# A Fourier-mixing kernel with its start-up rearranged: an early table piece, fewer dummy matmuls, filter loads on GpSimd's queue, and filter halves exchanged by ScalarE

## The chip, the cores and the metric

The kernel runs on one core of a Trainium2 chip. The metric is the device time of one execution in microseconds (us). Before the change it is 2619.39 us, the median of three runs between 2618.38 and 2620.06 us. TensorE is called PE below, VectorE DVE, ScalarE ACT, GpSimd POOL, and SyncE, which only issues transfers here, SP. Each of SP, ACT and POOL has a queue of its own for the transfers that it issues.

## The reference

The input x holds 8 batches of 3008 rows of 256 channels, all in float32. Each channel of a batch is transformed along its rows, multiplied by a complex filter and transformed back; the result then goes through a two-layer network with a hard-swish between the layers.

```python
X = np.fft.rfft(x, axis=1)                   # x: (8, 3008, 256)
Y = X * (filt_r + 1j * filt_i)[None, :, :]   # filters: (1505, 256)
a = np.fft.irfft(Y, n=3008, axis=1).reshape(24064, 256)
h = a @ w_in                                 # (256, 2048)
g = h * np.clip(h + 3.0, 0.0, 6.0) / 6.0
out = g @ w_out                              # (2048, 256)
```

## The kernel before

The transform of length 3008 is split as 47 times 64. It is done with matmuls: a first step over one factor (for batch 0 `a0_unit`), a second step over the other (`b_unit`), the product with the filters (`f_unit` and `y_unit`), and the way back (`bi_unit`, and after it `n_first` or `n_unit`). The network runs in 47 blocks of 512 tokens, and each block in 8 steps over slices of the 2048 inner columns. The work of batches 1 to 7 is fitted into the steps of the blocks by an explicit plan; only batch 0 is transformed by itself ahead of the first block. The order of every instruction on each engine is the order in which the program is written (`manual_schedule`), and each engine carries out its own in that order. What is changed lies in the stretch ahead of the first block, so that stretch is told here in its order.

1. Loads and dummies (lines 967 to 1026). While the first pieces of x are under way, PE runs two dummy matmuls on a tile of zeros (`keep_warm(2)`; each is one 128x512 float32 product, two passes in the trace). x of batch 0 comes in six pieces (`x0_load`), the table of the first transform step in four (`w0_load`); all go on SP's queue but the table's first piece, which goes on ACT's. Into the same row of SP's queue go the raw words of the weights (`load_bits`: the weights come as 64-bit floats and are converted to float32 on the chip) and then the filters (`table_load`, eight transfers each: four for the real and four for the imaginary part), the tables `wf` and `wi` and the identity matrix for transposes. Transfers share eight completion semaphores in rotation, so that a transfer is issued only when the eighth transfer before it has landed.
2. First transform step (lines 1027 to 1033). Eight times `a0_unit(j)`, for j = 0, 4, ... 28: each is 32 matmul passes on PE, whose results ACT and DVE copy out (from j = 24 on, ACT alone). Ahead of every second unit DVE makes the table's odd half from the even one (`w0_odd`, line 402), and that unit's matmuls wait for it. After j = 4, 12 and 20 come two dummy matmuls each. After j = 24 the first slice of weights is converted (`convert`: eight DVE operations, lines 310 to 338).
3. Six rounds, c = 0 to 5 (lines 1045 to 1058). A round has a `b_unit` on PE, two `f_unit`s on DVE (number 2c and 2c+1), the transposes of the next round (`turn(c + 1)`, on PE, copied out by ACT at line 398), and a `bi_unit` on PE for the pair of the round before, copied out by ACT and stored. An `f_unit` is three multiplications of 128x512 or 64x512 elements on DVE: the spectrum by the filter (line 548), and for the crossed products each half of the spectrum by the other half's filter (lines 549 and 550), since the real filter lies in partitions 0 to 63 and the imaginary one in 64 to 127. In the last round each `f_unit` is followed by a `y_unit`, two additions on DVE. The filters of rounds 0 and 1 lie in tiles of their own (`ft`), those of rounds 2 to 5 in pieces of the space that x of batch 0 took: rounds 2 and 3 in that of x's j = 0 to 7, rounds 4 and 5 in that of j = 8 to 15.
4. From the last round to the first block. `direct(10)` and `direct(11)` are 32 matmul passes of 470 or 94 columns each (line 719) on the results of the last two `y_unit`s; `bi_unit`, `n_first` and ACT's copies give the first tokens, and the first block begins (`plain_up`, line 859). Meanwhile DVE and ACT convert more slices of weights (`convert(3)`, `w_abs`), and go on with it through the first block, of which POOL then forms sums of weight blocks (`w_sums`, line 346).

Of the kernel before, what the change touches and what calls it, by code (L numbers as in the profile page):

```python
# [10 lines left out]
FP32 = mybir.dt.float32  # L11
I32 = mybir.dt.int32
AXT = mybir.ActivationFunctionType
ALU = mybir.AluOpType
# [17 lines left out]
P = 128  # L32
D = 256
B = 8
DFF = 2048
HALF = 64
# [6 lines left out]
TC = 4  # L43
NT = KH // TC
TB = 3
FB = 2
# [127 lines left out]
def kernel(  # L174
# [9 lines left out]
    nc = tc.nc  # L184
# [6 lines left out]
    wf_d = nc.inline_tensor(wf_np, name="wf_t").ap()  # L191
# [9 lines left out]
    def pool(name, bufs, **kw):  # L201
        return ctx.enter_context(tc.tile_pool(name=name, bufs=bufs, **kw))
# [12 lines left out]
    op = pool("op", 2)  # L215
    psF = pool("psF", 2, space=PSUM)
    psU = pool("psU", 1, space=PSUM)
# [3 lines left out]
    wf = const.tile([P, 4, 64], FP32, name="wf")  # L221
# [9 lines left out]
    ft = [ft_all[:, ts(i, TC), :] for i in range(FB)]  # L231
# [8 lines left out]
    st = {}  # L240

    def raw(src, row, ap):
        return bass.AP(tensor=src.tensor, offset=src.offset + row * D, ap=ap)


    def table_load(b, c):
        n = TC if b or c < FB else 2 * TC
        if n == TC:
            t = ft[(b * NT + c) % FB]
            st["ft", b, c] = t  # L250
        else:
            t = x0_at(2 * TC * D * (c // 2 - 1), 2 * TC * D).rearrange("p (k d) -> p k d", k=n)
            for i in range(2):
                st["ft", b, c + i] = t[:, ts(i, TC), :]
        for src, p0 in ((filt_r, 0), (filt_i, HALF)):
            for r in range(2):
                o = p0 + 32 * r
                nc.sync.dma_start(t[o:o + 32:2, :, :].rearrange("p k d -> p (k d)"),
                                  raw(src, c * TC + NA * r, [[2 * NA * D, 16], [1, n * D]]))
                nc.sync.dma_start(t[o + 1:o + 32:2, :, :],  # L260
                                  raw(src, NA * (2 - r) - c * TC, [[2 * NA * D, 16], [-D, n], [1, D]]))

    NCONV = 16

# [16 lines left out]
    def w_before(i):  # L281
        same = [j for j in range(i) if W_AT[j] == W_AT[i]]
        return same[-2] if len(same) > 1 else -1
# [13 lines left out]
    def w_abs(i):  # L297
        words = st["bits", i].rearrange("p (n two) -> p n two", two=2)
        st["high", i] = sp.tile([P, 512], FP32, name="s1")
        nc.scalar.activation(out=st["high", i], in_=words[:, :, 1].bitcast(FP32), func=AXT.Abs)  # L300
        nc.scalar.activation(out=words[:, :, 0].bitcast(FP32), in_=words[:, :, 0].bitcast(mybir.dt.uint32), func=AXT.Copy, scale=2.0 ** -32)
# [75 lines left out]
    def x0_at(o, n):  # L377
        return w_all.rearrange("p a b c m -> p (a b c m)")[:, ds(NP * 14 * P - HC * D + o, n)]
# [5 lines left out]
    def w0_load(j, n, q):  # L384
        o = 1 + j * ATOM if j else 0
        q.dma_start(w0[X0:XR, o:1 + (j + n) * ATOM], w0_d[X0:XR, o:1 + (j + n) * ATOM])

    def x0_load(j, n):
        nc.sync.dma_start(x0[X0:XR, j:j + n, :].rearrange("p j d -> p (j d)"), raw(x[0], j, [[HC * D, XR - X0], [1, n * D]]))

    def zt(dh):
        return (xn.rearrange("p a c n -> p (a c n)"), xs.rearrange("p i j d -> p (i j d)"))[dh]

    def copy(dve, to, ps):
        if dve:
            nc.vector.tensor_copy(out=to, in_=ps)
        else:
            nc.scalar.activation(out=to, in_=ps, func=AXT.Copy)

    def w0_odd(j, n):  # L400
        e = w0[0:XR, ds(1 + j * ATOM, n * ATOM)]
        nc.vector.tensor_scalar(out=w0[0:XR, ds(1 + (HC + j) * ATOM, n * ATOM)], in0=e, scalar1=w0[0:XR, 0:1],
                                scalar2=1.0, op0=ALU.mult, op1=ALU.mult)
# [10 lines left out]
    def turn(c):  # L414
        t = t2p.tile([P, TC, D], FP32, name="t2")
        for v in range(2):
            ps = psU.tile([P, 512], FP32, name=("al", "be")[v])
            for s_ in range(2):
                for dh in range(2):
                    z = zt(dh).rearrange("p (s r x) -> p s x r", s=2, x=NU)[:, s_, 2 * c + v, :]  # L420
                    nc.tensor.transpose(ps[:, ds(s_ * D + dh * P, P)], z, st["start"][:, 0:P])
            copy(False, t[:, 2 * v:2 * v + 2, :].rearrange("p k d -> p (k d)"), ps)
        st["t2", 0, c] = t.rearrange("p (v s) d -> p v s d", v=2)


# [113 lines left out]
    def f_unit(b, i):  # L539
        c, r = divmod(2 * i, TC)  # L540
        ps = st.pop(("ps", b, i))
        f = st["ft", b, c][:, r:r + 2, :]

        pool_, n1, n2 = (hp, "h0", "h1") if b == 0 and i & 2 else (sp, "s1", "s2")
        s1, s2 = (pool_.tile([P, 512], FP32, name=n).rearrange("p (u d) -> p u d", u=2) for n in (n1, n2))

        re, im = slice(0, HALF), slice(HALF, P)
        nc.vector.tensor_tensor(out=s1, in0=ps, in1=f, op=ALU.mult)
        nc.vector.tensor_tensor(out=s2[re], in0=ps[re], in1=f[im], op=ALU.mult)
        nc.vector.tensor_tensor(out=s2[im], in0=ps[im], in1=f[re], op=ALU.mult)  # L550
        st["y", b, i] = s1, s2

    def y_unit(b, i):
# [61 lines left out]
    def g_store(b, i):  # L615
        t = st.pop(("t3", b, i))
        for v in range(2):
            nc.gpsimd.dma_start(g_d[b, :, :, ds(2 * (i + v), 2), :].rearrange("c ri u d -> c ri (u d)"),
                                t[ts(v, 64)].rearrange("p ri u d -> p ri (u d)"))
# [4 lines left out]
    for b in range(B):  # L624
# [4 lines left out]
        n = 0  # L629
# [12 lines left out]
    def pair(i):  # L642
        b, js, o, n = chunks[i]
        return b * HC * NA + o, n
# [65 lines left out]
    def direct(i):  # L710
        if "psn" not in st:
            st["psn"] = {(c, dh): (psO.tile([P, 2, 2, P], FP32, name="po%d" % (2 + dh)).rearrange("p a u m -> p (a u m)")
                                   if c else psF.tile([P, 512], FP32, name="psn", tag="f"))
                         for c in range(2) for dh in range(2)}
        for u in range(2):
            k = 2 * i + u - KH + TC
            for (c, dh), ps in st["psn"].items():
                t, n = c * NJ * TOK, (1 if c else NJ) * TOK
                nc.tensor.matmul(ps[:, 0:n], st["y", 0, i][:, u, ts(dh, P)], st["direct"][k][:, ds(t, n)],
                                 start=k == 0, stop=False, skip_group_check=True)  # L720
# [207 lines left out]
    for b in range(B):  # L928
        for n, m, na in (((0, 6, NA), (6, 16, NA), (22, 9, NA)) if b == 0 else ((0, 16, NA), (16, 15, NA)) if b < B - 1
                         else ((0, 16, NA), (16, 10, NA), (26, 1, SPLIT))):  # L930
            o = b * HC * NA + n * NA
# [35 lines left out]
    with tc.manual_schedule():  # L967
# [16 lines left out]
        def load_bits(most):  # L984
            nonlocal loaded
            while loaded < most and w_before(loaded) < done:
                w_load(loaded, nc.sync)
                loaded += 1

        def convert(n):  # L990
            nonlocal done
            for i in range(n):
                w_conv(done)
                w_conv_2(done)
                done += 1
# [13 lines left out]
        ps = psU.tile([P, 512], FP32, name="al")  # L1009

        def keep_warm(n):
            for i in range(n):
                nc.tensor.matmul(ps, zero[:, P:2 * P], zero, start=True, stop=True)

        keep_warm(2)
        for j, n in (0, 4), (4, 4), (8, 8), (16, 8), (24, 4), (28, 4):
            if j % 8 == 0:
                w0_load(j, 8, nc.sync if j else nc.scalar)
            load_bits(j == 28)
            x0_load(j, n)  # L1020
        nc.sync.dma_start(st["start"][:, 0:P], start_d)
        table_load(0, 0)
        nc.sync.dma_start(wf, wf_d)
        nc.sync.dma_start(wi, wi_d)
        table_load(0, 1)
        load_bits(2)
        for j in range(0, HC, 4):
            if j % 8 == 0:
                w0_odd(j, 8)
            a0_unit(j)  # L1030
            if j in (4, 12, 20):
                keep_warm(2)
            convert(j == 24)
        nc.gpsimd.memset(t4, 0.0)
        for c in range(FB, NT, 2):
            table_load(0, c)
# [8 lines left out]
        for c in range(NT):  # L1045
            for i in (2 * c, 2 * c + 1):
                if i % 2 == 0:
                    b_unit(0, i)
                f_unit(0, i)
                if c == NT - 1:  # L1050
                    y_unit(0, i)
            if c + 1 < NT:
                turn(c + 1)
            if c:
                bi_unit(0, 2 * c - 2)
                (g0_first if c == NT - 1 else lambda i: g_store(0, i))(2 * c - 2)
            if c == 4:
                first_load(0, KH - 3 * TC)
        first_load(KH - 3 * TC, KH - TC)
        for i in 1, 2:  # L1060
            w_abs(i)
        direct(NU - 2)
        direct(NU - 1)

# [17 lines left out]
        half = 0  # L1082
# [28 lines left out]
        for i in range(2, len(chunks)):  # L1111
            k = pair(i)[0] // PAIRS
# [70 lines left out]
        for i in range(len(items) + 1):  # L1183
            up = i < len(items)
            k, p = items[min(i, len(items) - 1)]
# [98 lines left out]
```

## Time and profile before

One profiled execution took 2620.5 us, 1.1 us more than the median of the runs; its span is 2618.7 us.

| Engine | busy, us | share of the span |
|---|---|---|
| PE | 2594.3 | 99% |
| DVE | 2054.6 | 78% |
| ACT | 1291.4 | 49% |
| POOL | 485.6 | 19% |

These shares are averages over stages with different limits. The stretch that the change touches is the first 75 us of the span or so; there the table below counts more than the one above. It comes from the view of the profile by stretches.

| Stretch, us | PE busy | DVE busy | ACT busy | granted PE clock |
|---|---|---|---|---|
| 6.70 to 12.20 | 0.00 | 0.01 | 0.00 | 0.79 |
| 35.00 to 43.00 | 7.31 | 7.56 | 3.41 | 1.00 |
| 43.00 to 51.00 | 8.00 | 7.70 | 4.55 | 1.00 |
| 79.00 to 100.00 | 21.00 | 20.03 | 12.42 | 1.00 |

A matmul's busy time in the trace is modelled, so a PE that is busy throughout need not be the limit; whether it is has to be read from the waits and from the order of time. "Idle before, releaser" in a row of the trace names what the engine had waited for.

### The profile page before, as it was taken

The page shows a single profiled execution, that of the slowest core. Times are in us where ns is not written, and L with a number is a line of the kernel's source. Part 1 is how long each engine was busy: PE and PEld are TensorE (multiplying, and loading weights), DVE is VectorE, ACT ScalarE, POOL GpSimd, SP SyncE. Part 2 cuts the span into 40 slices and gives each one's busy share as a digit, 9 for nine tenths or more (in the row PEclk, how much of TensorE's full clock was granted, in tenths as well). Part 3 has the DMA queues.
Part 4 walks back from the last instruction along what each step waited for, and adds up shares of the span by engine and source line. Part 5 has one row for each costly group of instructions (what it writes and reads, how often), then busy time and mean ns, then how long its engine had stood idle before and what let it go on. Part 6 is the DMA issues. An engine that isn't in the chain of part 4 may idle for free.

```text
span 2618.7 us, 87007 instructions
## 1 busy us (share of the span) xinstructions
PE 2594.3 (99%) x37896; PEld 2044.6 (78%) x37896; DVE 2054.6 (78%) x3616; ACT 1291.4 (49%) x2678; POOL 485.6 (19%) x711
## 2 busy tenths in 40 slices
PE   7999999999999999999999999999999999999999
PEld 4477777778877788788877878778787788888887
DVE  6978867888778886888868888788877888766666
ACT  3554455444544455444554544544445454455554
POOL 2161122111121112211122121211112120111110
PEclk9999999999999999999999999999999999999999
DMA  7742243212332123421224113341133321110000
GB/s 210 216 118 68 57 110 109 66 35 70 88 109 70 33 76 82 113 66 33 84 75 122 56 33 86 79 117 54 40 80 88 109 57 48 51 44 20 23 22 26
DMA packets 130419, 199.25 MB, mean 76 GB/s; under 512 B 21698, under 2 KB 97952, under 8 KB 129718
## 3 DMA queue, kind: packets, MB, share of 16 engines
q1 hardware_dynamic: 114925, 149.15, 20.3%
q0 software_dynamic: 14720, 44.16, 6.1%
q8 instruction: 297, 4.87, 0.8%
q14 instruction: 84, 0.69, 0.1%
q10 hardware_dynamic: 393, 0.39, 0.1%
HBM read 121.35 MB, written 83.98 MB: 78 GB/s over the span
## 4 chain that ended last, share of the span: by engine, by line
PE 93%; DVE 3%; POOL 1%; issue 0%; DMA 0%; ACT 0%; SPq 0%; POOLq 0%; DVEq 0%; ACTq 0%
PE po L752 43%; PE al L752 24%; PE be L752 18%; PE psn L692 2%; PE psf L528 1%; PE psf L469 1%; PE psf L587 1%; PE be L587 1%; POOL w_all L346 1%; PE be L469 1%; DVE g L805 1%; DVE y L312 0%; PE psn L752 0%; DVE y L335 0%; DVE w_all L338 0%
## 5 line engine op out<-in xcount | busy, mean ns | idle before, releaser
L752 PEld LDWEIGHTS po<-w_all,g 128*64 128x64 f32 x20808 | 1232.5, 137 | 247.0 <-issue 12.8
L752 PE MATMUL po<-w_all,g 128*64 128x128 f32 (+1 forms) x20808 | 1406.9, 274 | 1.4 <-DVE g L805 0.7
L800 ACT ACTIVATE r<-h,half_c 128x512 f32<-128x512 f32 x736 | 531.0, 722 | 345.1 <-DVE h L781 333.0
L752 PE MATMUL al<-xt,w_all 128*64 128x256 f32 x4416 | 664.1, 379 | 2.4 <-POOL w_all L346 2.3
L805 DVE SCALAR_TENSOR_TENSOR g<-r,h 128x512 f32<-128x512 f32 x736 | 535.6, 729 | 143.6 <-ACT r L800 128.5
L752 PE MATMUL be<-xt,w_all 128*64 128x256 f32 x2944 | 442.6, 379 | 0.0
L781 DVE TENSOR_TENSOR h<-be,s 128x512 f32<-128x512 f32 x368 | 254.0, 690 | 132.3 <-PE be L752 101.9
L747 POOL TENSOR_TENSOR xt<-xn 128x256 f32<-128x256 f32 x184 | 150.5, 837 | 892.5 <-ACT xn L674 892.5
L752 PEld LDWEIGHTS be<-xt,w_all 128*64 128x64 f32 x2944 | 211.2, 137 | 106.5
L752 PEld LDWEIGHTS al<-xt,w_all 128*64 128x64 f32 x4416 | 278.9, 137 | 3.7 <-POOL w_all L346 3.4
L795 ACT ACTIVATE h<-al 128x256 f32<-128x256 f32 x368 | 141.0, 383 | 274.5 <-PE al L752 273.1
L813 DVE TENSOR_TENSOR g<-g 128x512 f32<-128x512 f32 x367 | 261.3, 712 | 12.6
L786 DVE TENSOR_TENSOR h<-al,s 128x256 f32<-128x256 f32 x368 | 156.1, 424 | 137.8 <-PE al L752 132.8
L776 ACT ACTIVATE s<-al 128x256 f32<-128x256 f32 x368 | 141.3, 384 | 207.5 <-PE al L752 207.5
L752 PE MATMUL al<-xn,w_all 128*64 128x256 f32 (+1 forms) x1536 | 240.1, 393 | 1.1 <-DVE g L805 0.7
L752 PE MATMUL be<-xn,w_all 128*64 128x256 f32 (+1 forms) x1536 | 236.4, 388 | 0.0
L767 ACT ACTIVATE s<-be 128x256 f32<-128x256 f32 x368 | 141.1, 383 | 170.2 <-PE be L752 170.2
L812 DVE TENSOR_TENSOR g<-g 128x256 f32<-128x256 f32 x367 | 165.4, 451 | 12.5
L766 ACT ACTIVATE s<-al 128x256 f32<-128x256 f32 x368 | 141.4, 384 | 59.3 <-PE al L752 59.3
L818 DVE TENSOR_TENSOR g<-g 128x256 f32<-128x256 f32 x367 | 162.4, 442 | 2.4
L752 PEld LDWEIGHTS be<-xn,w_all 128*64 128x64 f32 x1536 | 110.3, 137 | 62.3 <-issue 7.1
L494 POOL DMA_DIRECT2D z_tmp<-t x144 | 71.8, 506 | 321.6 <-ACT s L767 296.0
(159 smaller groups left out, 1763.4 us busy)
## 6 DMA issues: line engine op xcount, KB each, us to landing
t<-g_tmp SPq DMA_DIRECT2D x184, 120.0 KB
t<-z_tmp SPq DMA_DIRECT2D x42, 512.0 KB
g_tmp<-t POOLq DMA_DIRECT2D x68, 256.0 KB, 4.3
z_tmp<-t POOLq DMA_DIRECT2D x120, 144.0 KB, 3.3
o_tmp<-o SPq DMA_DIRECT2D x46, 256.0 KB
xs<-in_x_dram SPq DMA_DIRECT2D x60, 192.0 KB
ft<-in_filt_r_dram SPq DMA_DIRECT2D x176, 64.0 KB
ft<-in_filt_i_dram SPq DMA_DIRECT2D x176, 64.0 KB
```

The source lines that it names most:

```text
L747: nc.gpsimd.tensor_tensor(out=o, in0=x0, in1=x1, op=op_)
L752: nc.tensor.matmul(ps[ds(o, STRIP)], w[:, ds(o, STRIP)], x, skip_group_check=True, **kw)
L766: nc.scalar.activation(out=s[:, 0, :], in_=al, func=AXT.Copy)
L767: nc.scalar.activation(out=s5, in_=be[:, 1, :], func=AXT.Copy)
L776: nc.scalar.activation(out=s[:, 1, :], in_=al, func=AXT.Copy)
L781: nc.vector.tensor_tensor(out=st["h"][0].rearrange("p (a n) -> p a n", a=2), in0=be, in1=s, op=ALU.add)
L786: nc.vector.tensor_tensor(out=st["h"][1][:, 256:512], in0=al, in1=s5, op=ALU.add)
L800: nc.scalar.activation(out=r, in_=st["h"][i], func=AXT.Relu, bias=half_c, scale=1.0 / 6.0)
L805: nc.vector.scalar_tensor_tensor(out=st["g", k, p][:, o:o + 2, :].rearrange("p a n -> p (a n)"), in0=st["r", i], scalar=1.0, in1=st["h"][i ...
L812: v.tensor_tensor(out=g[:, G1, :], in0=g[:, G3, :], in1=g[:, G22, :], op=ALU.add)
L813: v.tensor_tensor(out=g[:, G3:G2 + 1:2, :], in0=g[:, G3:G1 + 1, :], in1=g[:, G11:G11 + 1, :].broadcast_to([P, 2, 256]), op=ALU.subtract)
L818: nc.vector.tensor_tensor(out=g[:, G4, :], in0=g[:, G12, :], in1=g[:, G2, :], op=ALU.subtract)
```

## The change

There are six edits.

- The table's first piece goes on SP's queue, ahead of all of x, instead of on ACT's.
- The first raw weights are asked for ahead of x's fifth piece instead of its sixth, and their conversion stands after `a0_unit(20)` instead of after `a0_unit(24)`. `wf` is asked for ahead of the first filters instead of after them.
- The dummy matmuls after j = 4 and 12 are one each instead of two, those after j = 20 are gone, and one stands after j = 24. Two new ones stand ahead of `direct`.
- The imaginary filters of rounds 2 to 5 are loaded through POOL's queue, and the filters of rounds 2 and 3 now take the space of x's j = 16 to 23.
- Of round 0's two copies after the transposes, DVE makes the second.
- For rounds 4 and 5 ACT copies the filters with their halves exchanged into the `ft` tiles that rounds 0 and 1 have left (`swap`, in rounds 2 and 3), and their `f_unit`s then need one multiplication of 128x512 in place of the two of 64x512.

```diff
@@ table_load
-            t = x0_at(2 * TC * D * (c // 2 - 1), 2 * TC * D).rearrange("p (k d) -> p k d", k=n)
+            t = x0_at(2 * TC * D * (3 - c // 2), 2 * TC * D).rearrange("p (k d) -> p k d", k=n)
...
         for src, p0 in ((filt_r, 0), (filt_i, HALF)):
+            q = nc.gpsimd if p0 and n > TC else nc.sync
             for r in range(2):
                 o = p0 + 32 * r
-                nc.sync.dma_start(t[o:o + 32:2, :, :].rearrange("p k d -> p (k d)"),
+                q.dma_start(t[o:o + 32:2, :, :].rearrange("p k d -> p (k d)"),
...
+    def swap(c, half):
+        f, t = st["ft", 0, c], ft[c % FB]
+        st["tf", 0, c] = t
+        for o in half:
+            copy(False, t[ds(HALF - o, HALF), :, :], f[ds(o, HALF), :, :])
@@ turn
-            copy(False, t[:, 2 * v:2 * v + 2, :].rearrange("p k d -> p (k d)"), ps)
+            copy(c == 0 and v == 1, t[:, 2 * v:2 * v + 2, :].rearrange("p k d -> p (k d)"), ps)
@@ f_unit
         nc.vector.tensor_tensor(out=s1, in0=ps, in1=f, op=ALU.mult)
-        nc.vector.tensor_tensor(out=s2[re], in0=ps[re], in1=f[im], op=ALU.mult)
-        nc.vector.tensor_tensor(out=s2[im], in0=ps[im], in1=f[re], op=ALU.mult)
+        if ("tf", b, c) in st:
+            nc.vector.tensor_tensor(out=s2, in0=ps, in1=st["tf", b, c][:, r:r + 2, :], op=ALU.mult)
+        else:
+            nc.vector.tensor_tensor(out=s2[re], in0=ps[re], in1=f[im], op=ALU.mult)
+            nc.vector.tensor_tensor(out=s2[im], in0=ps[im], in1=f[re], op=ALU.mult)
@@ the stretch ahead of the first block
-                w0_load(j, 8, nc.sync if j else nc.scalar)
-            load_bits(j == 28)
+                w0_load(j, 8, nc.sync)
+            load_bits(j == 24)
             x0_load(j, n)
         nc.sync.dma_start(st["start"][:, 0:P], start_d)
+        nc.sync.dma_start(wf, wf_d)
         table_load(0, 0)
-        nc.sync.dma_start(wf, wf_d)
...
             a0_unit(j)
-            if j in (4, 12, 20):
-                keep_warm(2)
-            convert(j == 24)
+            if j in (4, 12, 24):
+                keep_warm(1)
+            convert(j == 20)
...
+            if c in (2, 3):
+                swap(c + 2, (0, HALF))
...
+        ps = psU.tile([P, 512], FP32, name="al")
+        keep_warm(2)
         direct(NU - 2)
         direct(NU - 1)
```

## The prediction

> **What bounds the kernel now.** First the page: its chain of work that ended last is PE for 93%, nearly all in the network. The six edits lie in the first 62 us, so what counts is whether time won there reaches the point from which PE runs without a break. I read the timeline of that stretch, the table by stretches, the waits, and the chain up to 200 us.
>
> ```profile
> PE 93%; DVE 3%; POOL 1%; issue 0%; DMA 0%; ACT 0%; SPq 0%; POOLq 0%; DVEq 0%; ACTq 0%
> ...
> DVE w_all L402 <- DMA w_all<-w_t: 7.7, 1, 7.7
> ...
> 6.70:12.66 5.96, 0.00 (x1) 0.00 (x1) 0.42 (x1) 0.00 (x0) 2.39 (x2) 0.77 1.03 244
> 12.66:17.39 4.73, 4.73 (x65) 4.61 (x65) 0.56 (x1) 0.98 (x2) 0.00 (x0) 0.57 1.03 275
> ```
>
> The first line is the page's chain, the second a wait, the others rows by stretch (PE, weight loads, DVE, ACT, POOL, granted clock, DMA share, GB/s). PE idles 6 us because DVE waits 7.7 us for the table's first piece, and then starts at clock 0.57.
>
> ```profile
> 12.66 4.80 PE L752 MATMUL po<-w_all 112*64 112x96 f32 x64 [5.96 <-DVE w_all L402]
> 17.39 1.98 PE L1013 MATMUL al<-r 128*128 128x512 f32 x4
> 19.30 2.86 PE L752 MATMUL po<-w_all 112*64 112x96 f32 x64
> ...
> 55.90 0.69 DVE L550 TENSOR_TENSOR s<-po,w_all 64x512 f32<-64x512 f32 x1
> 56.63 0.69 DVE L548 TENSOR_TENSOR h<-po,w_all 128x512 f32<-128x512 f32 x1
> 57.35 0.68 DVE L549 TENSOR_TENSOR h<-po,w_all 64x512 f32<-64x512 f32 x1
> 58.05 0.69 DVE L550 TENSOR_TENSOR h<-po,w_all 64x512 f32<-64x512 f32 x1
> 58.77 0.69 DVE L559 TENSOR_TENSOR t<-h 64x512 f32<-64x512 f32 x1
> 59.49 0.69 DVE L560 TENSOR_TENSOR t<-h 64x512 f32<-64x512 f32 x1
> ```
>
> In the timeline, two units of the first step cost 4.80 us cold and 2.86 warm, a warm dummy pair 1.98, and PE has no gap until the transposes at 31.50. The rounds are DVE's: three multiplications at a pitch of 0.715 us, without a gap, six per round (4.29 us; PE needs 4.10).
>
> ```profile
> 57.72:60.28 2.56, 0.00 (x0) 0.03 (x1) 2.45 (x5) 0.60 (x1) 0.00 (x0) 1.00 0.49 130
> 60.28:63.56 3.28, 3.28 (x8) 1.92 (x9) 3.17 (x5) 2.34 (x4) 0.00 (x0) 0.62 0.31 74
> 63.56:66.05 2.49, 2.49 (x9) 1.43 (x9) 2.28 (x5) 0.00 (x0) 0.00 (x0) 0.81 0.88 180
> 66.05:68.08 2.03, 2.03 (x11) 1.21 (x10) 1.96 (x4) 0.00 (x0) 1.13 (x2) 1.00 1.05 378
> ...
> 75.23 0.69 DVE L331 TENSOR_TENSOR y<-g,y 128x512 f32<-128x512 f32 x1 [2.03 <-ACT g L301]
> ...
> 130.67 36.46 POOL L346 TENSOR_TENSOR w_all<-w_all 128x128 f32<-128x128 f32 x64 [16.38 <-DVE w_all L338]
> ```
>
> PE waits 2.56 us for `y_unit(10)`, its clock drops, and the four equal quarters of `direct` take 3.28, 2.49, 2.03 and 2.11 us. At 75.23 DVE waits for ACT, which is behind PE's end of `direct`; from there DVE converts weights almost without a gap to 130.5, POOL's 64 subtractions follow that, and then PE. So a shift of the end of `direct` passes to the end of the kernel.
>
> **The change part by part**, on the profiled execution's 2620.5 us.
>
> *Start of the first step.* The trace's landing events show x's first two pieces at 5.3 and 6.6 us, x's j = 8 to 15 at 11.2, j = 16 to 23 at 14.8, the table's fourth piece at 15.4, the raw weights at 18.6, x's last at 20.1; the table's first piece, 3% of the bytes, came at 12.3. Put first, it lands near 4, and the other pieces move by at most its 0.6 us (148 KB at 244 GB/s). Units 0 and 4 then start when the first dummies end, at 6.7. From there: unit 8 at 11.3 (its x), units 8 and 12 2.86, one dummy 0.95, units 16 and 20 2.86: PE is done at 18.0.
>
> *The moved conversion.* In the changed program's order on DVE its eight operations stand ahead of `w0_odd(24)`, which stood ahead of them before. DVE's copy ends at 18.5; the raw weights, now one piece earlier, land at 17 to 18; the eight operations took 27.72 to 32.11, 4.39 us; `w0_odd` 0.41. So unit 24 starts at 23.3 although its x is there by 19: PE idles 5.3 us, and the nearest rows (idle 5.96, then 0.57) say that it resumes cold. Units 24, dummy, 28 cost 1.43 + 0.95 + 1.43 = 3.8 us warm, 2.40 + 1.84 + 2.40 = 6.6 cold (the cold pair of dummies at 3.02 took 3.68). Before, the clock was back 4 to 5 us after PE resumed, so I take 2.40 + 1.84 + 1.4 = 5.6. The transposes start at 28.9 instead of 31.5: -2.6 us, between -1.6 and -4.4.
>
> *DVE's copy in round 0.* ACT's second copy starts 0.50 after its first and takes 0.60; DVE's of that shape takes 0.69 and can start no earlier: +0.1. DVE is free there.
>
> *The exchanged halves.* Four steps lose a multiplication; three of them lie ahead of `y_unit(10)`: 3 x 0.715 = -2.1 us at `direct`'s start. Step 11 wins a fourth, but its result (63.8 before) is needed only halfway through `direct`. ACT pays four copies of 64x1024: by its rows of 256 columns (0.384) and 512 (0.597) each is 1.02 us. In rounds 2 and 3 they add 2.04 to some 2.3 us of copies, against a round of 4.29. Behind them on ACT stand the transposes' copies, for which `b_unit` waits; these come 0.9 us later than before, but `b_unit` ran 3 us ahead of DVE in rounds 4 and 5. Cost nothing; without that cover up to 2 us.
>
> *Filters on POOL's queue.* Eight issues leave SP (0.64 each, 5.1 us), and what follows there is asked for that much earlier. POOL had nothing between 9.1 and 42.1; by its issue rows of 0.5 to 0.65 us its eight are done within 6 us of unit 20's end, and the nearest landings, 3 to 6 us, put the filters there by 30. `swap` wants them at 43, `f_unit(4)` at 41. Nothing, and at most 1 us either way by contention. `wf` and the raw weights' place in the queue: nothing, wanted 10 us later.
>
> *Dummies.* Those after 4, 12 and 24 are in the sums above; the pair after 20 lay on the path and is in the difference. The two ahead of `direct` start when the last round's `bi_unit` ends, 1.4 us ahead of `y_unit(10)`'s new end, and run 1.9: `direct` starts at most 0.5 later, 0.1 by the timeline. If they keep the clock, `direct` takes four times 2.03 instead of 9.91: -1.8 us (between -1.8 and 0).
>
> The Trainium skill ("TensorE: Matmul & The Clock Gate", section "HAM oscillation — how this bites in real kernels") wants no PE gap of over about 3.4 us. By that the gap of 2.56 us would throttle nothing, the pair would be worth nothing, and the sum would be 1.8 us smaller; the clock of 0.62 behind that gap says otherwise, and I go by it.
>
> *What is late next.* On DVE alone 75.23 could move by 2.5 + 2.9 + 2.03 = 7.4 us, on the way over PE and ACT by 2.6 - 0.1 + 2.1 - 0.1 + 1.8 = 6.3; the smaller holds. Raw weights for the following conversions landed 5 to 10 us before use, and the transfers for `n_first` 4.8 us ahead, of which 2.4 are used up.
>
> Sum: 2620.5 - 6.3 = 2614.2 for such an execution; it stood 1.1 above the median, so 2613.1 for the median.
>
> **Rivals.** *Nothing of the start is left.* PE stays cold to the transposes, or the filters on POOL's queue delay the conversion: the first term shrinks to -1 or less, and the direct pair brings half: -3.5, 2615.9. For it: the 5.3 us hole is the change's own. Against it: eight microseconds of slack on x's last piece before.
>
> *The gain is lost on the way.* From 64 to 72 the DMA engines are 100% busy; if the loads behind `direct` set the pace, only half arrives: -3, 2616.4. Against it: no wait for a load of raw weights shows before 79.
>
> *More at the start.* The clock survives or returns at once: 3.8 instead of 5.6, and the total is -8.1: 2611.3.
>
> *Slower: the clock stays down in the rounds.* With fewer dummies PE comes cold out of the hole and the rounds' gaps keep it so. A round of 4.10 at 4.80/2.86 is 6.9 us, 2.6 over DVE's; five rounds cost 13, against 6.3: +7, 2626. It decides once the share of PE's work in a round (62% between 31.50 and 34.00, with clock 1.00) is too little to lift the clock from cold. Against it: it was lifted at 17 while PE worked without a break, as it does from 23.3.
>
> **How the numbers follow.** Forecast 0.60 (2611.8 to 2614.8 for its own terms), more at the start 0.12, start lost 0.09, lost on the way 0.09, slower 0.10. Likeliest 2613.1. The range runs from 2610.5, below the better start, to 2617, above both lost cases. About 0.2%, 5.2 us, is what a measurement can tell: the limit is 2614.2. Of the forecast about a seventh lies above it, of the lost cases nearly all: faster 0.65, same 0.25, slower 0.10.
>
> **What would show it.** After: the wait for the table's first piece gone and units 0 and 4 at about 6.7; PE idle from 18 to 23 behind `w0_odd`; transposes at about 28.9; two multiplications a step in rounds 4 and 5, four ACT copies of about 1.0 us; `direct` near 8.1 us with clock 1.00; POOL's 64 subtractions at about 124.4 instead of 130.67. I'm wrong if ACT waits for filters in `swap`, if PE's clock is below 1 in the rounds, or if the start of POOL's subtractions moves much less than the end of `direct`.

## The result: 2614.8 us, and the profile after

The changed kernel takes 2614.78 us (median of 20 runs between 2613.59 and 2616.06). The kernel before took 2619.06 on the same chip (20 runs between 2617.88 and 2620.49). The ratio is 0.9983 with a 95% interval from 0.9976 to 0.9990: 4.3 us won, 0.17%. The two profiled executions lie further apart, 2620.5 and 2613.62, which is 6.9 us; what the traces suggest for that difference stands further down. The page's chain of work that ended last, after:

```profile
PE 96%; DMA 2%; DVE 1%; SPq 0%; issue 0%; ACT 0%; POOL 0%; POOLq 0%; DVEq 0%; ACTq 0%
```

DVE's share of the chain fell from 3% to 1%. The table by stretches of the changed kernel has PE, weight loads, DVE, ACT and POOL with their busy time, then the granted clock, the DMA share and GB/s:

```profile
17.64:23.18 5.54, 0.00 (x2) 0.03 (x1) 5.06 (x10) 0.00 (x0) 4.70 (x8) 0.71 1.09 226
23.18:28.89 5.71, 5.71 (x66) 4.38 (x66) 0.00 (x0) 1.47 (x3) 0.00 (x0) 0.68 0.94 185
31.50:53.50 22.00, 21.28 (x176) 9.17 (x176) 20.15 (x30) 14.14 (x23) 4.56 (x8) 1.00 0.86 263
...
55.63:63.80 8.17, 8.17 (x34) 4.81 (x32) 7.65 (x14) 2.38 (x4) 0.00 (x0) 1.00 0.50 131
```

PE idles 5.54 us behind the moved conversion (the hole, in what follows) and comes back at a clock of 0.68 (first two lines). In the rounds the clock is 1.00, and so it is in `direct` (last line), where it had been 0.62 and 0.81 in the first two quarters. The timeline of the same execution:

```profile
6.57 2.86 PE L762 MATMUL po<-w_all 112*64 112x96 f32 x64
...
22.46 0.41 DVE L409 TENSOR_SCALAR w_all<-w_all 112x384 f32<-112x384 f32 x1
23.18 2.83 PE L762 MATMUL po<-w_all 112*64 112x96 f32 x32 [5.54 <-DMA ft<-in_filt_i_dram]
...
43.49 2.13 ACT L405 ACTIVATE ft<-w_all 64x1024 f32<-64x1024 f32 x2
...
53.81 1.98 PE L1023 MATMUL al<-r 128*128 128x512 f32 x4
55.63 1.74 PE L729 MATMUL psn<-w_all,t 128*128 128x470 f32 x4
...
124.08 36.40 POOL L353 TENSOR_TENSOR w_all<-w_all 128x128 f32<-128x128 f32 x64 [16.21 <-DVE w_all L345]
```

Units 0 and 4 run at 6.57 instead of 12.66. Unit 24 (23.18) is cold and takes 2.83 us, because `w0_odd(24)` comes only at 22.46, behind the eight operations of the conversion. The releaser that the line names, a filter transfer, isn't it: unit 24 multiplies what `w0_odd` wrote, and starts 0.3 us behind its end, as it does (0.2 us) in the other kernels with this order. POOL's 64 subtractions start at 124.08 instead of 130.67.

Where the time went in this pair of executions, as shifts of the same landmark: first transpose 31.50 to 28.89 (-2.61); end of `y_unit(10)` 60.18 to 55.02 (-5.16); end of `direct` 70.20 to 63.80 (-6.40); end of POOL's subtractions 167.13 to 160.48 (-6.65); span -6.9. So in this pair what is won ahead of the first block arrives, and nothing in the 2450 us behind it gives any back.

### The profile page after: what moved, and what is told of

Its sections match the earlier page's. It is cut to its first block, busy times and chain, and to the rows that moved or that the text cites. A ratio compares the mean times of both kernels' runs of the same rounds, so it can differ in the third digit from the quotient of the medians.

```text
span 2611.8 us, 87014 instructions
## 1 busy us (share of the span) xinstructions
PE 2590.7 (99%) x37894; PEld 2042.8 (78%) x37894; DVE 2050.0 (78%) x3613; ACT 1294.1 (50%) x2681; POOL 491.1 (19%) x719
## 4 chain that ended last, share of the span: by engine, by line
PE 96%; DMA 2%; DVE 1%; SPq 0%; issue 0%; ACT 0%; POOL 0%; POOLq 0%; DVEq 0%; ACTq 0%
PE po L762 44%; PE al L762 25%; PE be L762 18%; PE psn L702 2%; PE psf L535 1%; PE psf L476 1%; PE psf L597 1%; PE be L597 1%; DMA w_all<-in_x_dram 1%; PE be L476 1%; PE psf L581 0%; DMA out_dram<-o 0%; PE psf L762 0%; PE psf L449 0%; DVE g L815 0%
```

## The experiments

My theory was the prediction's sum: the start, the exchanged halves and the dummies ahead of `direct` bring some 2 us each, and the hole ahead of unit 24 costs some. The rivals were that the halves or the dummies bring nothing by themselves, that the hole costs nothing because the filters are late anyway, and that POOL's queue carries part of the gain. In the table each kernel stands beside the kernel before on the same chip, in runs taken in turn with its own.

| Kernel | median us (runs) | before, same chip | difference | ratio, 95% interval |
|---|---|---|---|---|
| changed kernel | 2614.78 (20) | 2619.06 | -4.3 | 0.9976 to 0.9990 |
| conv24 | 2612.06 (8) | 2619.45 | -7.4 | 0.9962 to 0.9982 |
| hole_warm | 2614.31 (11) | 2619.45 | -5.1 | 0.9971 to 0.9988 |
| no_direct_dummies | 2614.90 (11) | 2619.45 | -4.6 | 0.9972 to 0.9990 |
| table_first | 2616.35 (11) | 2619.45 | -3.1 | 0.9979 to 0.9997 |
| no_swap | 2617.29 (11) | 2619.77 | -2.5 | 0.9980 to 0.9997 |
| no_swap_no_dummies | 2619.06 (11) | 2619.77 | -0.7 | 0.9987 to 1.0004 |
| sp_filters | 2615.65 (11) | 2619.77 | -4.1 | 0.9975 to 0.9993 |
| imag_all_pool | 2615.28 (11) | 2619.77 | -4.5 | 0.9973 to 0.9991 |
| conv24_nod | 2611.75 (7) | 2620.02 | -8.3 | 0.9959 to 0.9981 |
| best2 | 2610.10 (5) | 2620.02 | -9.9 | 0.9951 to 0.9978 |
| best3 | 2608.76 (5) | 2620.30 | -11.5 | 0.9943 to 0.9970 |

The intervals reach 2 to 3 us to either side, so a difference of 1 to 3 us between two of the changed kernels is read from the landmarks in their traces; the medians alone can't settle it. two_halves, with a single run, is not in the table.

Unless it says otherwise an edit is made to the changed kernel.

### conv24: the conversion back behind unit 24

```diff
-            convert(j == 20)
+            convert(j == 24)
```

> The changed kernel, but the first conversion again behind a0_unit(24), so that w0_odd(24) stands ahead of it on DVE. If the moved conversion makes the hole in PE (17.64 to 23.18 us), unit 24 starts when its x has landed, at 19.3 us, unit 28 at about 21, the transposes at about 23 instead of 28.9; f_unit(0) is then held by the first filters, which land at 27.9, and starts at 28 instead of 32.7: about 4.2 us less than the changed kernel, some 2610.5. If it is the late x or the transfers that make the hole, unit 24 stays at 23 and the time at 2614.8.

The hole is gone, and the kernel is about 3 us faster than the changed one by the medians (-7.4 beside -4.3, with intervals that overlap); in its trace POOL's subtractions start 2.4 us earlier (121.70 against 124.08). The timeline shows what came in its place:

```profile
19.54 1.54 PE L762 MATMUL po<-w_all 112*64 112x96 f32 x32 [1.65 <-DMA w_all<-in_x_dram]
...
29.03 0.69 DVE L555 TENSOR_TENSOR s<-po,ft 128x512 f32<-128x512 f32 x1 [2.95 <-DMA ft<-in_filt_r_dram]
...
41.30 2.13 ACT L405 ACTIVATE ft<-w_all 64x1024 f32<-64x1024 f32 x2 [1.92 <-DMA w_all<-in_filt_r_dram]
```

Unit 24 starts at 19.54 as its x lands, warm. The transposes come at 23.53 instead of 28.89, 5.4 us earlier, but `f_unit(0)` starts only 3.7 us earlier: it now waits 2.95 us for filters. `swap` waits 1.92 us for filters too, and from `f_unit(0)` to the end of `y_unit(10)` it takes 23.43 us instead of 22.31. So the hole cost something, less than its length, and less than the 4.2 us expected here.

### table_first: one edit alone, on the kernel before

```diff
-                w0_load(j, 8, nc.sync if j else nc.scalar)
+                w0_load(j, 8, nc.sync)
```

> The kernel before, with only the table's first piece put at the head of SP's queue. Units 0 and 4 start at 6.6 us, the transposes at about 23.6 instead of 31.5; f_unit(4) then waits for the filters of rounds 2 and 3, which landed at 38.4 before: all in all some 5.2 us less than the kernel before, 2613.9. By the forecast's account of the start (2.6 us with the moved conversion) this one edit is worth more than in the changed kernel; if the rival holds that the start's gain is lost on the way, the time stays within 1 us of 2619.1.

This line alone brings 3.1 us by the medians, beside the change's 4.3, where 5.2 had been expected. The pair of traces does show 5.3 at the start of POOL's subtractions (125.35 against 130.67), but this trace is one of the fastest runs of its kernel, and the one before stands above its median. The transposes come at 24.02, 7.5 us earlier than before the change, against 2.6 with all six edits. Part of it is lost again to a wait for filters in the second round, in DVE's timeline:

```profile
38.46 0.69 DVE L548 TENSOR_TENSOR s<-po,w_all 128x512 f32<-128x512 f32 x1 [2.21 <-DMA w_all<-in_filt_r_dram]
```

### hole_warm: five more dummies in the hole

```diff
             a0_unit(j)
+            if j == 20:
+                keep_warm(5)
```

> The changed kernel with five more dummy matmuls after a0_unit(20), some 4.8 us of work in PE's hole. If the slow clock behind the hole is what makes units 24 and 28 and their dummy take 5.7 us, they take 3.8 us with clock 1.00 and everything after comes 1.9 us sooner: 2612.9. If the clock does not matter there (copies or transfers set the pace), nothing changes. If the clock's own phase is what spreads the runs of one kernel by 2.5 us, the spread gets smaller.

Units 24 and 28 run warm: from the start of unit 24 to the transposes it takes 4.00 us, with clock 1.00, instead of 5.71. But unit 24 itself started at 24.16 instead of 23.18 in this execution, so the transposes come at 28.16 instead of 28.89. Beside the kernel before, the median is only 0.8 lower than the changed kernel's, which can't be told from nothing, and the spread is no smaller (2612.55 to 2615.80). In its profile the clock drops at another place, at 145.7 us; the section on the hardware comes back to that.

### no_direct_dummies: the pair ahead of direct taken out

```diff
-        ps = psU.tile([P, 512], FP32, name="al")
-        keep_warm(2)
         direct(NU - 2)
```

> The changed kernel without the two dummy matmuls ahead of direct. By the forecast's term direct takes 9.9 us instead of 8.17 and starts 0.5 us sooner: +1.2 to +1.8 us in a profiled run, 2616.3. If the drop of the clock seen before the change hangs on where the gap falls in the clock's own period, only part of the runs pay: +0.5 us in the median and a wider spread. If the drop was chance, 0.5 us faster.

The median is the same (2614.90 and 2614.78). In the table by stretches, the wait ahead of `direct` and `direct` itself:

```profile
55.30:56.56 1.26, 0.02 (x3) 0.04 (x1) 1.20 (x3) 0.60 (x1) 0.00 (x0) 1.00 1.00 249
56.56:64.80 8.24, 8.24 (x34) 4.88 (x34) 7.78 (x13) 2.39 (x4) 0.00 (x0) 1.00 0.41 107
```

`direct` keeps a clock of 1.00 and takes 8.24 us without any dummy. PE's wait ahead of it is 1.26 us here, and was 2.56 before: the exchanged halves had already shortened it.

### no_swap and no_swap_no_dummies: without the exchanged halves

```diff
-            if c in (2, 3):
-                swap(c + 2, (0, HALF))
```

and, in the second, also the edit of no_direct_dummies. The results are computed in the old way, with three multiplications a step.

> The changed kernel without the exchanged halves: rounds 4 and 5 have three multiplications a step again. If they are worth 0.95 us a step (2.145 against 1.20 us, as the changed kernel's rows stand), the end of y_unit(10) moves by 2.8 us, but direct started 0.6 us after it and now follows at once: 2.3 us slower, 2617.1. If they are worth the forecast's 0.715 a step, 1.6 us slower, 2616.4. The two dummies now fill a gap of 2.6 us; direct takes 8.2 us.

> The changed kernel without the exchanged halves and without the two dummies ahead of direct. If the dummies' gain hangs on the length of the gap, the gap of 2.6 us drops the clock in a part of the executions: in a profile where it does, direct takes 9.9 us instead of 8.2, and the median is 0.5 to 1.5 us above the run without the halves alone, while without the dummies alone it cost nothing (gap 1.3 us). If the forecast's account is right and the dummies as such bring 1.8 us, it is 1.8 us slower than the run without the halves alone.

`y_unit(10)` ends 28.82 us behind the first transpose in no_swap and 26.12 in the changed kernel, 2.7 us or 0.90 a step; the medians give 1.8. Without the halves the wait ahead of `direct` is back, and there the dummies bring 1.8 us by the medians and 1.3 in the two traces. In the timeline of the kernel with neither:

```profile
59.42 2.17 PE L729 MATMUL psn<-w_all,t 128*128 128x470 f32 x4 [2.56 <-issue]
...
62.18 2.75 PE L729 MATMUL psn<-w_all,t 128*128 128x470 f32 x4
...
65.19 1.77 PE L729 MATMUL psn<-w_all,t 128*128 128x470 f32 x4
```

Behind 2.56 us of idle time the groups of 470 columns take 2.17, 2.75 and then 1.77 us, and `direct` 9.91. So each of the two edits alone kept `direct` warm in its trace; the second adds nothing.

### two_halves: what the exchanged halves save

```diff
-            nc.vector.tensor_tensor(out=s2, in0=ps, in1=st["tf", b, c][:, r:r + 2, :], op=ALU.mult)
+            for h_ in re, im:
+                nc.vector.tensor_tensor(out=s2[h_], in0=ps[h_], in1=st["tf", b, c][h_, r:r + 2, :], op=ALU.mult)
```

> The changed kernel, but in rounds 4 and 5 the multiplication of 128x512 by the exchanged filters is split into two of 64x512, each with both operands in the same partitions. If the pitch of 0.72 us came from the crossed partitions of the kernel before, the two go at 0.60 us and y_unit(10) ends 0.6 us per step later than in the changed kernel, near 56.9 for three steps. If it comes from operations that use half the partitions, they go at 0.72 and it ends near 57.9, and with the 58.1 of the kernel without exchanged halves. The view to read is the pitch of the multiplications in rounds 4 and 5.

Its one run took 2618.12 us, and `y_unit(10)` ends at 57.63, near the second of the two values. DVE's timeline:

```profile
50.16 0.69 DVE L555 TENSOR_TENSOR s<-po,w_all 128x512 f32<-128x512 f32 x1
50.77 1.38 DVE L558 TENSOR_TENSOR s<-po,ft 64x512 f32<-64x512 f32 x2
52.18 0.69 DVE L555 TENSOR_TENSOR s<-po,w_all 128x512 f32<-128x512 f32 x1
```

The first half follows the full multiplication after 0.61 us, the second half its predecessor after 0.69, and the next full one after 0.73: 2.02 a step, against 2.14 before and 1.20 with one multiplication. Neither theory is right as I put it: the first half has half the partitions and yet comes after 0.61, and the second has aligned operands and comes after 0.69.

### sp_filters: all filters on SP's queue again

```diff
-            q = nc.gpsimd if p0 and n > TC else nc.sync
+            q = nc.sync
```

> The changed kernel with all filters on SP's queue. The filters of rounds 4 and 5 are asked for up to 41.4 us and land at about 44, and the exchange on ACT, which began at 43.5, waits up to 1 us; b_unit runs 3 us ahead, so the forecast's nothing holds: within 0.5 us of 2614.8. If the cover is too thin: ACT's wait comes through, up to 2 us slower.

4.1 us beside 4.3, and from `f_unit(0)` to the end of `y_unit(10)` 22.32 us beside 22.31: POOL's queue brings nothing that these runs can tell.

### imag_all_pool: all imaginary filters on POOL's queue, on top of conv24_nod

```diff
-            q = nc.gpsimd if p0 and n > TC else nc.sync
+            q = nc.gpsimd if p0 else nc.sync
-            convert(j == 20)
+            convert(j == 24)
-        ps = psU.tile([P, 512], FP32, name="al")
-        keep_warm(2)
```

> The first conversion behind a0_unit(24), no dummies ahead of direct, and all imaginary filters on POOL's queue, those of rounds 0 and 1 too. With the conversion moved alone, f_unit(0) waited 2.95 us and the exchange on ACT 1.92 us for filters. If SP's row of filter issues is what delays them, both waits go or shrink below 1 us and the time falls by 1 to 2 us to about 2610.5; if the bytes as such set the pace (x's last piece comes later instead), it stays at 2612.

It is 3.8 us slower than conv24_nod when each stands beside the kernel before on its own chip. Two things went wrong. POOL's `memset` of a tile, which runs at 7.08 in the changed kernel, now stands behind eight DMA issues, and beside it DVE's `w0_odd(8)` takes 3.58 us instead of 0.41, from the timeline (the three first lines). And the edit also caught the filters of later batches, whose eight issues, 4.1 us, now stand in the middle of POOL's subtractions (the three last):

```profile
10.16 3.58 DVE L409 TENSOR_SCALAR w_all<-w_all 112x384 f32<-112x384 f32 x1
...
11.26 2.25 POOL L1044 MEMSET t<- 128x2560 f32 x1
...
13.95 1.39 PE L762 MATMUL po<-w_all 112*64 112x96 f32 x14 [3.26 <-POOL t L1044]
...
122.25 4.84 POOL L353 TENSOR_TENSOR w_all<-w_all 128x128 f32<-128x128 f32 x9 [16.21 <-DVE w_all L345]
127.04 0.52 POOL L259 DMA_DIRECT2D ft<-in_filt_i_dram  x1
...
131.12 31.78 POOL L353 TENSOR_TENSOR w_all<-w_all 128x128 f32<-128x128 f32 x55
```

The subtractions end at 162.91, 4.5 us later than in conv24 (158.37), although they begin only 0.55 later.

### conv24_nod, best2 and best3: what the experiments point to

conv24_nod joins the edits of conv24 and no_direct_dummies. best2 adds the imaginary filters of rounds 0 and 1 on POOL's queue, for batch 0 alone and behind those of rounds 2 and 3 (one load of four transfers), which wait for unit 20 (`table_load` gets an argument for which of the two filters it loads):

```diff
-            q = nc.gpsimd if p0 and n > TC else nc.sync
+            q = nc.gpsimd if p0 and b == 0 else nc.sync
...
-        table_load(0, 0)
+        table_load(0, 0, (0,))
...
-        table_load(0, 1)
+        table_load(0, 1, (0,))
...
-        for c in range(FB, NT, 2):
-            table_load(0, c)
+        table_load(0, FB)
+        for c in range(FB):
+            table_load(0, c, (1,))
+        table_load(0, FB + 2)
```

best3 issues only the first of these four transfers ahead of those of rounds 0 and 1, and the other three behind them.

> The changed kernel with the conversion of the first weights back behind a0_unit(24) and without the two dummies ahead of direct. If those dummies only delay direct by half a microsecond (direct started 0.62 us behind y_unit(10) with them and 0.10 without), it should come out at 2611.6, 0.5 below the 2612.06 with the dummies. If they do keep the clock up when PE comes without the hole ahead of the rounds, direct takes up to 1.8 us more and the time is about 2613.4. The view to read is the granted clock in direct: 1.00 by the first, below by the second.

> As the run above, and the imaginary filters of rounds 0 and 1 go through GpSimd's queue too, but behind those of rounds 2 and 3, which wait until unit 20 has left its x; so they cannot compete with x's earlier pieces, and the real filters of round 0 have four transfers less ahead of them or between them on SyncE's queue. With the order of the queue as the cause of the 2.95 us wait of f_unit(0), that wait shrinks to 1 us or less and f_unit(0) starts at 27.2 instead of 29.0: 2610.0, 1.6 below the run above. With the bytes as the cause (the 16 queues are busy for 0.86 to 1.09 of that stretch) f_unit(0) stays at 29, and the time at 2611.6, or later where the imaginary filters now come last. The view to read is the first multiplication of f_unit(0) and what it waits for.

> The version at 2610.1 with another order on GpSimd's queue: one transfer of the imaginary filters of round 2 first (it waits for unit 20, and holds the queue until then), then the imaginary filters of rounds 0 and 1, then the rest of round 2. In that version those of round 0 were issued from 20.93 us on, and f_unit(0) started at 27.94 behind a wait of 2.50; here they are issued some 2.5 us earlier. If their place in the queue sets f_unit(0), it starts near 25.8 and the time is about 2608.3 beside 2610.1. If the bytes set it (the queues are busy throughout, and the real filters and the next raw weights come in the same stretch), f_unit(0) stays within 0.5 us of 27.9 and the time at 2610. The view to read is the first multiplication of f_unit(0) and the waits of the six units behind it.

The three medians came within 0.5 us of what was expected: 2611.75, 2610.10 and 2608.76. In conv24_nod `direct` ran with clock 1.00 in 8.24 us. From the first transpose to `f_unit(0)` it is 5.49 us in conv24, 5.04 in best2, which still waits 2.50 us for a transfer, and 3.81 in best3, as in the changed kernel, where PE alone set it (3.81). The start of `f_unit(0)` does not decide between the two accounts by itself: 27.48 is within the 0.5 us of 27.9 that stood for the bytes. The landings do. The last of the four transfers of round 0's imaginary filter lands at 27.57 in best2, and the wait ends with it; in best3 it is issued 0.6 us earlier and lands at 25.17. So its place in the queue was the cause. In best3 that wait is no longer one for a transfer (the first line is best2's, and the raw weights that it names aren't what `f_unit(0)` needs; the others are best3's, DVE and PE):

```profile
27.94 0.69 DVE L555 TENSOR_TENSOR s<-po,ft 128x512 f32<-128x512 f32 x1 [2.50 <-DMA bits<-in_moe_w_out_dram]
```

```profile
27.48 0.69 DVE L557 TENSOR_TENSOR s<-po,ft 128x512 f32<-128x512 f32 x1 [1.27 <-PE po L537]
...
61.11 1.84 PE L764 MATMUL psn<-wai,t 128*64 128x94 f32 x40 [1.17 <-DMA t<-g_tmp]
```

`f_unit(0)` now waits for PE, not at 25.8 as expected but at 27.48, since unit 4 started at 9.04 in this execution and 7.68 in best2's. And there is a new wait: `n_first` waits 1.17 us for the tokens' way through memory, which the prediction had seen 4.8 us ahead; `direct` ends 11.4 us earlier than before by now. best3 is the fastest version measured, 11.5 us under the kernel before and 6 to 7 under the changed one, though its interval and best2's overlap.

## Why the prediction was right, point by point

The likeliest time was 2613.1, the range 2610.5 to 2617.0, and 2614.78 lies inside it. It lies just outside the limit of 0.2% (2614.2): the kernel is faster, since the interval lies wholly below 1, but by less than the bound that "faster", with 0.65, was given for, and inside the one of "same", with 0.25. On the pair of profiled executions the sum, -6.3, stands beside a shift of `direct`'s end of -6.40. That it comes so near is luck in part: two terms were mis-sized, in opposite directions (+0.6 us on the halves, -0.4 on the start of `direct`), and the 1.8 us of the dummies came by another edit.

- **Start, -2.6.** In the pair -2.61, with the hole of 5.54 us (5.3 forecast), the cold unit 24, and the transposes at 28.89 (28.9). The four other kernels that are the same up to there had the transposes at 29.15, 29.31, 30.32 and 30.49 (sp_filters, the same but for the queue of the filters, at 30.48). The median of the first five is 29.31, so about -2.2 is typical, inside the range given; how much the start of the kernel before varies is not known, since it has one trace. The landing times in the prediction stand some 0.25 us late against the timeline (DVE's wait for the table's first piece, put at 12.3, had ended by 12.19), so that unit 8, forecast at 11.3, ran at 10.74; at unit 24 0.1 us of it was left.
- **DVE's copy in round 0, +0.1.** From the transposes to `f_unit(0)` 3.68 before, 3.81 after: +0.13.
- **Halves, 3 x 0.715 = -2.1.** This is the first term that was mis-sized. It measured 2.7 in the traces: a step goes from 2.14 to 1.20 us. What failed is "three multiplications at a pitch of 0.715 us": I took the pitch as a property of each multiplication, and it isn't, as the last section shows. The cover of ACT's copies held; two take 2.13 us, and no `b_unit` came late for them.
- **Filters on POOL's queue: nothing.** sp_filters agrees, within what its runs can tell.
- **Dummies ahead of `direct`, -1.8.** This is the second. `direct` went from 9.91 to 8.17 us as forecast, but the step "If they keep the clock, `direct` takes four times 2.03 instead of 9.91" gave the gain to the wrong edit. I had noted that the halves shorten PE's wait, and not asked what the clock does behind the shorter wait. no_direct_dummies shows that it stays at 1.00, and no_swap_no_dummies that without the halves the dummies would have earned most or all of their 1.8. In the changed kernel they only delay `direct`, which starts 0.62 us behind `y_unit(10)` (0.1 forecast).
- **What is late next.** The shift passed to POOL's subtractions whole (124.08; 124.4 forecast), and no load behind `direct` took it. That such a wait exists a few us further on, best3 shows.
- **From the pair to the median.** The forecast took off 1.1 us, since the profiled execution of before stood so far above its median. The executions differ by 6.9 us and the medians by 4.3: before's profile stands 1.4 above the median of the 20 runs and after's 1.2 below. The likeliest time is 1.7 us too low, most of it for this reason. The last section gives the cause that the traces point to.

Three of the rivals did not come: the clock was 1.00 in the rounds, the shift arrived whole, and the clock did not survive the hole. Of the fourth, "nothing of the start is left", a grain was true: table_first wins 7.5 us at the transposes, and the moved conversion gives back 5 of them. I had costed the hole only against the kernel before, where PE was late anyway, and so didn't see that the edit which makes it is the change's worst; taking it out was worth 2.4 us in the traces and 3 by the medians.

## What to carry to other kernels

Ask of each protective edit (dummies, a warm-up) what it protects against once the other edits of the same change have been made; the gap that it was for may be gone. When an edit frees an engine early, look for work moved into the freed time that now stands ahead of something on the path: here eight conversions ahead of one 0.4 us operation. And where two profiled executions differ by more than their medians do, look at where the clock's switches fall in each before sizing a term from the pair.

## What the runs showed of the hardware

**A multiplication on DVE waits for the end of the one before it only in some orders.** In rounds 4 and 5 of the changed kernel:

```profile
49.90 0.69 DVE L555 TENSOR_TENSOR s<-po,w_all 128x512 f32<-128x512 f32 x1
50.51 0.68 DVE L557 TENSOR_TENSOR s<-po,ft 128x512 f32<-128x512 f32 x1
51.10 0.68 DVE L555 TENSOR_TENSOR s<-po,w_all 128x512 f32<-128x512 f32 x1
51.70 0.68 DVE L557 TENSOR_TENSOR s<-po,ft 128x512 f32<-128x512 f32 x1
```

Each takes 0.68 to 0.69 us, yet they follow one another every 0.60 us, while the pitch among the rounds' multiplications was 0.69 to 0.73 wherever an operand or the output started at another partition than in the operation before (in every step of before and of no_swap, and behind the first half in two_halves). The Trainium skill ("VectorE: DVE Perf Modes", section "Two Vector instructions with no wait between them") gives it as a model that an instruction is held until all earlier ones have ended where its output or an input starts in another group of 32 partitions than that of the last instruction in the same memory did. The three pitches of two_halves, 0.61, 0.69 and 0.73, agree with that one by one: the first half starts at partition 0 as the full one did, the second half at 64, the next full one at 0 again. By this rule each step of the changed kernel saves one multiplication and two such holds, which fits 0.95 where I had 0.715.

**PE's clock is decided in fixed windows of 3.41 us, and where they fall differs from one execution to the next.** In each trace all switches of the granted clock lie a multiple of 3.41 us apart, and the first full clock came between 5.85 and 9.13 us in the fourteen traces, almost a whole window's spread. The Trainium skill ("TensorE: Matmul & The Clock Gate", section "What's actually happening") has a window of 3413 ns that runs on freely; the traces agree. The same page's rule against idle gaps of over about 3.4 us (section "HAM oscillation — how this bites in real kernels") does not hold here: shorter ones cost the clock too. I laid PE's gaps over the windows of their own trace:

| Trace | gap, us | idle inside one window | clock in the next window |
|---|---|---|---|
| conv24_nod | 139.93 to 142.88 | 2.95 | half |
| before | 57.72 to 60.28 | 2.56 | half |
| best3 | 138.62 to 140.99 | 2.37 | half |
| two_halves | 144.77 to 147.10 | 2.06 | half |
| conv24_nod | 17.63 to 19.64 | 2.01 | half |
| sp_filters | 143.94 to 145.96 | 1.99 | full |
| no_swap_no_dummies | from 17.91 on, the hole | 1.87 | half |
| conv24 | 139.96 to 142.28 | 1.77 | full |
| before | 148.77 to 151.04 | 1.21 | full |
| changed kernel | 142.35 to 144.18 | 1.29 | full |

So, with one exception, the clock fell where 2.01 us or more of one window were idle, and stayed where it was 1.99 or less, whatever the gap's whole length: one of 2.32 us split between two windows (conv24) cost nothing. Of all windows of the fourteen traces in their first 990 us that had a full clock and over 1.2 us idle, 31 in all, the one that does not fit is the 1.87 in the table; later such windows lie only at the kernel's end, and they fit. The limit is about 2 us, then, not sharper than that; PE's busy time is modelled. Two rows by stretches show it, cut at the windows' edges, best3 first and then sp_filters:

```profile
138.42:141.83 3.41, 1.04 (x16) 0.78 (x14) 0.84 (x2) 1.09 (x3) 3.16 (x8) 1.00 0.44 130
141.83:145.24 3.41, 3.41 (x33) 3.15 (x31) 2.19 (x5) 2.00 (x5) 3.17 (x7) 0.50 0.10 31
```

```profile
142.52:145.93 3.41, 1.42 (x22) 1.03 (x18) 0.08 (x1) 0.87 (x2) 3.17 (x8) 1.00 0.56 173
145.93:149.34 3.41, 3.38 (x48) 3.11 (x50) 3.05 (x6) 2.32 (x6) 3.17 (x7) 1.00 0.17 39
```

This gap near 143 us, behind POOL's subtractions, is in every version. In the traces in which the clock fell there (hole_warm, conv24_nod, two_halves, best3) the span's end lies 2453.8 to 2454.2 us behind the end of the subtractions, and in the others 2451.3 to 2452.1 (but 2449.9 in imag_all_pool, whose subtractions were interrupted): about 2.4 us by chance. The same chance is in the hole (transposes from 28.89 to 30.49), and in `direct` before: a gap of 2.56 us can have 2.0 of it inside one window for 0.85 + 0.56 + 0.56 = 1.97 of 3.41 positions, so an estimate is that some 6 in 10 executions paid its 1.8 us, and before's profiled one did. That would make the term worth about 1 us on average, the start's about 2.2, and the sum of the change 2.2 - 0.1 + 2.7 - 0.5 + 1.0 = 5.3, nearer to the measured 4.3 than 6.3 is; the last microsecond stays open. That the windows' position makes the spread of 2.5 us between runs of one kernel is argued from these traces; no experiment set it.

**An operation of DVE took nine times as long beside POOL.** In imag_all_pool `w0_odd(8)` took 3.58 us and ended at 13.74, 0.2 us behind POOL's `memset` of 11.26 to 13.51. Beside POOL's DMA issues alone, at 18 us in best2, the same operation took 0.41. A milder case is in every trace with the table first: `w0_odd(0)`, beside POOL's `memset`s of the first 7 us, takes 1.00 to 1.02 us (4.37 to 5.39 in the changed kernel). The `memset` itself took its usual time, 2.25 us against 2.23, so it was DVE that was held up. Why it was held already ahead of the `memset`'s start (0.41 us from 10.16 would have been enough) is not shown; the start and end of POOL's operations are rough in the traces.
